# The last batch's dense pieces brought forward in an attention-and-experts kernel on one Trainium2 core

## The chip, the cores and the metric

The kernel runs on one core of one Trainium2 chip. The metric is the device time of one execution in microseconds (us); less is better. The core has five engines that run side by side, each through its own queue of instructions in order: TensorE (PE, matmuls), VectorE (DVE), ScalarE (ACT), GpSimd (POOL, here also the issuer of indirect transfers) and SyncE (SP, here the issuer of plain transfers). They wait for one another through semaphores.

## What is computed

The reference is block-sparse attention followed by a layer of dense and routed feed-forward parts. The kernel's change lies wholly in the second half, which the reference gives as:

```python
h_dense = np.maximum(x @ w1_dense, 0.0)
y_dense = h_dense @ w2_dense
logits = x @ w_gate
expert_idx = np.argmax(logits, axis=1)
...
for e in range(E):
    mask = expert_idx == e
    ...
    h = np.maximum(x[mask] @ w1[e], 0.0)
    y_moe[mask] = gate_w[mask, None] * (h @ w2[e])
return (y_dense + y_moe).astype(np.float32)
```

`x` is the attention's output, 3072 tokens of 512 values, in 4 batches of 768 tokens. There are 8 experts with 512 by 512 weights each. Each token goes to the expert with the highest logit. All inputs are random float32 values.

## The kernel before

The attention phase goes through 16 pairs of heads, four for each batch, in units that are written out by hand. When a batch's attention is done, its feed-forward work is given out in small pieces, called fills, between the units of the next batch: transposes, the gate, the ranks of the tokens within their experts, the dense pieces, and the scattering of the rows (`place`, line 370) into a table in HBM that is sorted by expert. Every row of that table carries the token's 512 values in half precision, its gate weight and its number.

The last batch has no next batch to hide in. Its pieces are given out in the experts' phase, which starts at line 675 and is the part that is changed.

The experts' phase goes through blocks of 128 table rows that all belong to one expert. There are at most 31 blocks (`NBLK`); 28 of them (`NOFT`) are run without a condition and three more behind a condition at the end. The first 11 (`N1`) are full blocks of the first three batches, so they can start before the last batch is routed. The other ones, the second part, need the last batch's rows in the table. The loop over `i` does this for each block, in this order:

- it fetches the rows of later blocks (`fetch`, line 454, tile `xg`, 14 buffers), up to eight blocks ahead (`AHEAD`), but no block of the second part before block `READY`
- `e1(i)`, line 699: four matmuls with the expert's first weights, then a ReLU on ScalarE into `eh`
- `tx(i + 1)`, line 691: four transposes of the next block's rows, then a copy on VectorE into `exT`
- the pieces of the last batch that `extra` holds for this block
- `e2(i - 1)`, line 728: four matmuls with the second weights, the scaling by the gate weight on VectorE into `yo` (line 735, four buffers), and on GpSimd an indirect transfer (line 736) that adds the 128 rows to the output at their tokens
- `th(i)`, line 708: four transposes of `eh`, then a copy on ScalarE into `ehT`

The last block of the loop gets the rows of the output beforehand (`dense_rows`, line 720, tile `dr`), adds them on VectorE (line 733) and writes the sum without accumulation.

There are 14 dense pieces of the last batch, in the list `d`: four `l1` and three `l2` for the first half of the batch, then the same for the second half. An `l1` (line 385) is four matmuls of 384 columns and a ReLU on ScalarE into a quarter of `hT` (line 387). An `l2` (line 394) reads all four quarters of `hT` for 128 tokens, is copied by ScalarE to `ys` (line 397), and SyncE stores `ys` to the output in two transfers of 64 rows (line 400). These stores overwrite, while line 736 adds. So an add must come after the store of the same token. The code frees the adds of the first 11 blocks from that wait, since they hold no token of the last batch:

```python
if i < N1:
    tc.declare_no_dep(sc.ins, group="dense", reason="the first blocks hold no token of the last batch")
    tc.add_to_no_dep_group("add1", sc.ins)
```

The adds from block 11 on wait for all dense stores of the last batch.

SyncE also writes zero rows behind each expert's rows in the table (`empty`, line 751) and loads the starting rows of the second part's 20 possible blocks into registers (`load_rows`, line 434), which is done when the loop comes to block `READY`. It does all this, the fetches and the stores in one queue, in the program's order. The tile framework may move instructions a little against the order in which the lines are called, but each engine runs its own list in order.

Of the kernel before, what the change touches and what calls it, by code (L numbers as in the profile page):

```python
# [17 lines left out]
def kernel(  # L18
# [38 lines left out]
    N1 = (N * (B - 1) // B - E * 127 + 127) // 128  # L57
# [388 lines left out]
    def load_rows(n):  # L446
        rows.extend(registers(ro[:, len(rows) : n], mybir.EngineType.SP, EMPTY,
                              "blocks lie in their expert's rows, or are the empty one"))
# [3 lines left out]
    def fetch(i):  # L452
        es[i]["x"] = xg = eg.tile([128, XW], U16, name="xg")
        ld = nc.sync.dma_start(out=xg, in_=table[bass.ds(rows[i], 128)])  # L454
        if i < N1:
            tc.add_to_no_dep_group("full", ld.ins)
# [218 lines left out]
    with (  # L675
# [8 lines left out]
        a, d, ranks, places, _ = batch_fills(B - 1)  # L684

        wef = we.rearrange("p e j f -> p (e j f)")
        def tx(i):
            s = es[i]
            tp = p1.tile([128, NK, 128], HF, name="tp", tag="tr")
            for ko in range(NK):  # L690
                nc.tensor.transpose(tp[:, ko], s["x"][:, ko * 128 : (ko + 1) * 128].bitcast(HF), ident)  # L691
            s["xT"] = xT = et.tile([128, NK, 128], HF, name="exT")
            nc.vector.tensor_copy(xT, tp)  # L693
# [21 lines left out]
        def dense_rows(i):  # L715

            es[i]["dense"] = dr = et.tile([128, Dm], FP, name="dr", bufs=1)
            nc.vector.memset(dr, 0.0)
            with tc.issue_after(latest["pool"].ins):
                ga = nc.gpsimd.indirect_dma_start(out=dr, out_offset=None, in_=out, in_offset=tokens(i),  # L720
                                                  bounds_check=N - 1, oob_is_err=False)
            apart(ga, "add", "every token is in one block")
# [30 lines left out]
                tc.declare_no_dep(z.ins, group="full", reason="the first blocks end before these rows")  # L753

        AHEAD = 8
        READY = 4
        tx(0)
        extra = {0: a[:NT] + [a[NT], ranks], 1: places[:2], 2: places[2:4], 3: places[4:] + [empty]}
        for n, f in enumerate(d):
            extra.setdefault(1 + n * (N1 - 2) // len(d), []).append(f)  # L760
        got = FIRST

        RARE = 3
# [1 line left out]
        for i in range(NOFT):  # L765
            if i == READY:
                load_rows(NBLK)
            while got < min(i + AHEAD + 1, NOFT if i >= READY else N1):
                fetch(got)
# [10 lines left out]
            if i == NOFT - 4:  # L780
                dense_rows(NOFT - 1)
            if i == READY + 1:
                total = nc.values_load_multi_w_load_instructions(
# [41 lines left out]
```

## Time and profile before

| | |
|---|---|
| time, median of 3 runs | 254.45 us (253.21 to 255.98) |
| span of the profiled execution | 252.1 us |
| TensorE busy | 216.1 us (86%) |
| VectorE busy | 176.7 us (70%) |
| ScalarE busy | 177.8 us (71%) |
| GpSimd busy | 158.8 us (63%) |
| first matmul of the experts (line 699) | at 167.80 us |
| scatter-adds (line 736) | 28, 1.55 us each, 43.3 us in all |

Times are counted from the start of the span. A line of the timeline gives the start, the length, the engine, the line of the code, the operation, the tile that is written and the tile that is read, and in brackets how long the engine stood idle before it and what ended that. In the row of a DMA issue the length is the issuing alone; the data land later. A releaser named in brackets is inferred from semaphores, and where an instruction waits for several of them only the last is named. "issue" in the chain of waits is time in which the engine waited for nothing that the profile shows.

### The profile page before, as it was taken

What the parts mean: (1) busy time and instruction counts of PE and PEld (TensorE: products, weight loads), DVE (VectorE), ACT (ScalarE), POOL (GpSimd) and SP (SyncE); (2) the same over time, 40 slices, a digit from 0 to 9 for tenths busy, and PEclk for the clock granted to TensorE, in tenths of its full rate; (3) what the DMA queues carried; (4) which work ended last, traced back from release to release, by engine and by line L of the source; (5) the groups of instructions that cost most, each with busy time, mean ns of one, the idle gap of its engine ahead of it and who ended that gap; (6) DMA issues with size and microseconds to landing.
All of it is one profiled execution on the core that took longest, in us unless ns stands there. A gap on an engine that the chain in (4) does not pass through costs nothing. (4 is left out here: it accounts for less than half of the span.)

```text
span 252.1 us, 7252 instructions
## 1 busy us (share of the span) xinstructions
PE 216.1 (86%) x2547; PEld 142.4 (56%) x2547; DVE 176.7 (70%) x558; ACT 177.8 (71%) x332; POOL 158.8 (63%) x198
## 2 busy tenths in 40 slices
PE   1389879788999999899999998979999999989970
PEld 0256646666756677766667764536555454545530
DVE  6968989999979599998599995138533344356540
ACT  2699989887778999778899876834556554545540
POOL 4746998767386687378678345501787452688882
PEclk9999999999999999999999999999999999999995
DMA  6999999999999999999899925275599999579786
GB/s 178 264 267 233 217 225 260 214 181 249 260 197 261 197 274 204 232 205 285 187 299 201 216 47 166 72 188 162 130 287 144 239 263 257 84 130 130 100 132 116
DMA packets 75125, 50.13 MB, mean 199 GB/s; under 512 B 29648, under 2 KB 68176, under 8 KB 75088
## 3 DMA queue, kind: packets, MB, share of 16 engines
q1 hardware_dynamic: 59856, 30.33, 47.4%
q0 software_dynamic: 15232, 19.32, 45.6%
q8 instruction: 21, 0.34, 0.5%
q14 instruction: 16, 0.13, 0.2%
HBM read 41.93 MB, written 18.23 MB: 239 GB/s over the span
## 5 line engine op out<-in xcount | busy, mean ns | idle before, releaser
L558 ACT ACTIVATE ex<-sp 128x512 f16<-128x512 f32 (+1 forms) x176 | 90.8, 602 | 2.7 <-PE op L573 1.8
L554 PE MATMUL sp<-rT,kT 128*128 128x128 f16 (+3 forms) x384 | 63.8, 261 | 4.5 <-ACT ex L558 3.1
L736 POOL DMA_INDIRECT out_dram<-yo,xg x28 | 43.3, 1546 | 20.1 <-DVE yo L735 8.1
L560 POOL TENSOR_SCALAR_AFFINE_SELECT ex<-ex 128x512 f16<-128x512 f16 x48 | 32.1, 681 | 35.6 <-ACT ex L558 33.6
L573 PE MATMUL op<-v,ex 128*128 128x65 f16 x672 | 44.6, 194 | 2.2 <-POOL ex L560 1.7
L573 PEld LDWEIGHTS <-ex 128*128 128x128 f16 x672 | 34.8, 98 | 15.0 <-POOL ex L560 5.3
L735 DVE TENSOR_SCALAR yo<-yp,xg 128x512 f32<-128x512 f32 x27 | 20.3, 750 | 24.9 <-PE yp L728 15.3
L370 POOL DMA_INDIRECT table<-xbig,slot x24 | 24.0, 1000 | 20.1 <-issue 19.5
L554 PEld LDWEIGHTS <-kT 128*128 128x128 f16 x384 | 28.7, 98 | 7.9 <-issue 5.4
L498 DVE TENSOR_REDUCE ks<-kp 128x24 f16<-128x768 f16 x30 | 27.3, 943 | 5.0 <-ACT kp L487 4.8
L699 PE MATMUL hp<-we,exT 128*128 x112 | 29.2, 379 | 1.5 <-DVE exT L693 1.5
L710 ACT COPY ehT<-tp 128x512 f16<-128x512 f16 x28 | 16.4, 586 | 19.9 <-PE tp L708 19.9
L728 PE MATMUL yp<-we,ehT 128*128 x112 | 28.7, 379 | 0.8 <-ACTq L788 0.8
L385 PE MATMUL hp<-xT,wd 128*128 128x384 f16 x128 | 26.2, 325 | 1.5 <-DVE xT L258 0.4
L394 PE MATMUL yp<-wd,hT 128*128 128x512 f16 x96 | 24.3, 378 | 2.2 <-ACT ys L397 1.8
L702 ACT ACTIVATE eh<-hp 128x512 f16<-128x512 f32 x28 | 16.7, 597 | 12.6 <-PE hp L699 12.6
L693 DVE COPY exT<-tp 128x512 f16<-128x512 f16 x28 | 11.8, 422 | 14.4 <-PE tp L691 14.4
L397 ACT COPY ys<-yp 128x512 f32<-128x512 f32 x24 | 14.3, 596 | 9.4 <-PE yp L394 9.1
L387 ACT ACTIVATE hT<-hp 128x384 f16<-128x384 f32 x32 | 15.9, 497 | 6.9 <-PE hp L385 6.8
L487 ACT COPY kp<-pp 128x768 f16<-128x768 f16 x16 | 12.9, 807 | 9.9 <-PE pp L485 9.8
L385 PEld LDWEIGHTS <-wd 128*128 128x128 f16 x128 | 12.0, 97 | 9.9 <-issue 4.7
L584 DVE TENSOR_TENSOR xbig<-op,rs 128x384 f16<-128x384 f32 x32 | 17.4, 548 | 0.2
(127 smaller groups left out, 385.1 us busy)
## 6 DMA issues: line engine op xcount, KB each, us to landing
we<-in_moe_w_dram POOLq DMA_DIRECT2D x16, 512.0 KB, 8.9
kf<-in_k_dram SPq DMA_DIRECT2D x32, 192.0 KB, 4.7
qf<-in_q_dram SPq DMA_DIRECT2D x32, 192.0 KB, 5.5
vf<-in_v_dram SPq DMA_DIRECT2D x32, 192.0 KB, 7.4
out_dram<-ys SPq DMA_DIRECT2D x48, 128.0 KB, 4.7
xg<-table SPq DMA_DIRECT2D x28, 136.0 KB, 3.4
table<-zt SPq DMA_DIRECT2D x9, 136.0 KB, 4.5
wd<-in_moe_w_dense_dram POOLq DMA_DIRECT2D x2, 512.0 KB
```

The costliest lines, as they stand in the source:

```text
L370: sc = nc.gpsimd.indirect_dma_start(out=table, out_offset=bass.IndirectOffsetOnAxis(ap=keep["slot"][:, t : t + 1], axis=0), in_=xbig[b % 2 ...
L385: nc.tensor.matmul(hp, wd[:, ko, j * 128 : (j + 1) * 128], xT[:, ko, g * G * 128 : (g + 1) * G * 128], start=(ko == 0), stop=(ko == NK - 1))
L394: nc.tensor.matmul(yp, hold["h"][:, j, i * 128 : (i + 1) * 128], wd[:, NK + j], start=(j == 0), stop=(j == NK - 1))
L498: nc.vector.tensor_reduce(out=ks[:, i], in_=kp.rearrange("d (c w) -> d c w", w=32), op=op, axis=mybir.AxisListType.X)
L554: nc.tensor.matmul(sp[:, o : o + w], kT[p % NB][g][:, kt * 128 : (kt + 1) * 128], rT[p % NB][g][:, a * 128 : z * 128], start=(o == 0), sto ...
L558: nc.scalar.activation(ex[:, 0:o], sp[:, 0:o], AF.Exp, scale=-0.125)
L560: latest["pool"] = nc.gpsimd.affine_select(out=ex, in_=ex, compare_op=ALU.is_ge, fill=0.0, base=0, pattern=[[0, 4], [1, 2], [2, 64]], chan ...
L573: nc.tensor.matmul(s["op", g][:, t * (D + 1) : (t + 1) * (D + 1)], ex[:, o : o + 128], v16[p % NB][:, g, kt, :], start=first, stop=(last_o ...
L699: nc.tensor.matmul(hp, s["xT"][:, ko], wef[:, bass.ds(offs[i] + ko * 512, 512)], start=(ko == 0), stop=(ko == NK - 1))
L728: nc.tensor.matmul(yp, s["hT"][:, j], wef[:, bass.ds(offs[i] + (NK + j) * 512, 512)], start=(j == 0), stop=(j == NK - 1))
L735: nc.vector.tensor_scalar(o, yp, gate, None, ALU.mult)
L736: sc = nc.gpsimd.indirect_dma_start(out=out, out_offset=to, in_=o, in_offset=None, bounds_check=N - 1, oob_is_err=False, compute_op=ALU.by ...
```

## The change

Two numbers in the experts' phase are changed.

```diff
         AHEAD = 8
-        READY = 4
+        READY = 6
         tx(0)
         extra = {0: a[:NT] + [a[NT], ranks], 1: places[:2], 2: places[2:4], 3: places[4:] + [empty]}
         for n, f in enumerate(d):
-            extra.setdefault(1 + n * (N1 - 2) // len(d), []).append(f)
+            extra.setdefault(1 + n * (READY - 1) // len(d), []).append(f)
```

The 14 dense pieces were spread over blocks 1 to 9, one or two in each. With the new formula they lie in blocks 1 to 5: three in each of the first four and two in the fifth. The register load of the second part's rows and the fetches of its blocks come at block 6 instead of block 4 (and the load of the number of blocks, line 783, at block 7 instead of 5), so that in SyncE's queue they lie behind the dense stores. At block 6 the fetches of blocks 11 to 14 come together, where before blocks 11 and 12 came at block 4 and one more with each block. The purpose is to have the last batch's dense rows in the output before the first add that must wait for them.

## The prediction

> **What bounds the kernel now.** I read the chain of waits first. It does not leave the last part of the experts' phase: from 205 us on it runs through scatter-adds of block outputs and nothing else of weight.
>
> ```profile
> 205.52 7.16 DMA out_dram<-yo,xg
> 212.78 2.03 DMA xg<-table
> 214.91 0.49 issue
> ...
> 217.49 3.94 DMA out_dram<-yo,xg
> ...
> 234.22 12.58 DMA out_dram<-yo,xg
> 246.81 0.11 POOLq L788
> 246.92 0.93 POOL out_dram L736
> ```
>
> The reader is to see the hole between 205.52 and 215. Next I read GpSimd (POOL) alone in order of time. It issues one scatter-add per block, and block 10 is the row at 207.88.
>
> ```profile
> 205.52 1.55 POOL L736 DMA_INDIRECT out_dram<-yo,xg  x1 [0.62 <-DVE yo L735]
> 207.88 1.57 POOL L736 DMA_INDIRECT out_dram<-yo,xg  x1 [0.81 <-DVE yo L735]
> 215.63 1.56 POOL L736 DMA_INDIRECT out_dram<-yo,xg  x1 [6.18 <-DMA xg<-table]
> 217.49 1.55 POOL L736 DMA_INDIRECT out_dram<-yo,xg  x1 [0.30 <-issue]
> ...
> 239.80 1.07 POOL L720 DMA_INDIRECT dr<-out_dram,xg  x1 [0.30 <-issue]
> ...
> 246.81 1.03 POOL L736 DMA_INDIRECT out_dram<-yo,xg  x1 [0.30 <-DMA out_dram<-yo,xg]
> ```
>
> The add at 215.63 is block 11's, the first that the code does not exempt from the last batch's dense stores (`i < N1`, N1 = 11). Its 6.18 us are put down to a fetch; by the code it must wait for the last dense store. SyncE's (SP) queue in order of time shows when those stores go out, and the answer for line 434 its register loads (least, median and longest ns):
>
> ```profile
> 191.24 1.12 SPq L400 DMA_DIRECT2D out_dram<-ys  x2
> 192.61 0.93 SPq L454 DMA_DIRECT2D xg<-table  x2
> ...
> 203.20 3.60 SPq L400 DMA_DIRECT2D out_dram<-ys  x4
> 207.05 1.23 SPq L454 DMA_DIRECT2D xg<-table  x2
> 208.38 1.12 SPq L400 DMA_DIRECT2D out_dram<-ys  x2
> ```
>
> ```profile
> L434 SPq TENSOR_LOAD <-ro x2: 1620/4234/6849, 151.3 to 184.3; - x2
> ```
>
> The last store is issued before 209.5; such a store takes 4.7 us to land (median, 7.8 at most, the answer for line 400), so about 214 to 216: this is the wait. From 215.63 on GpSimd runs adds back to back, 1.86 us each, to the end. TensorE (PE) is the other near bound: it is busy 9.1 to 10.0 us of every 10 from 170 to 240. It loses time in the second part here:
>
> ```profile
> 209.42 0.38 PE L708 MATMUL tp<-ident,eh 128*128 128x128 f16 x4 [0.62 <-PE yp L728]
> 220.34 0.75 DVE L735 TENSOR_SCALAR yo<-yp,xg 128x512 f32<-128x512 f32 x1 [2.47 <-DMA out_dram<-yo,xg]
> 221.56 1.02 PE L699 MATMUL hp<-we,exT 128*128 x4 [0.87 <-DVE exT L693]
> ```
>
> The late add of block 11 keeps one of the four `yo` buffers; VectorE (DVE) stands behind it for 2.47 us, the next `exT` copy is queued behind that, and TensorE waits 0.87 us.
>
> **What the Trainium skill says.** "DMA: Bandwidth & Descriptors", section "Issuing engines are not separate DMA queues": transfers of all issuers share the same 16 engines and interleave. The trace agrees: the DMA share is 1.0 or more in most 2 us stretches from 182 to 214, and fetches that land in 2.1 us at best take 5 to 7.7 us there. "Runtime: NRT & Kernel Launch", section "Instruction fetch mechanics": a register load costs some 200 ns per register, which makes 4 us an estimate for the 20 of the second part. The trace differs both ways: 11 values took 1.62 us (147 ns each) with the DMA nearly idle, 20 took 6.85 us (342 ns each) in the saturated stretch. The measured pair is my bound: 2.9 to 6.85 us.
>
> **The change part by part.**
> *Dense pieces.* There are 14: eight `l1` (187.14 to 187.79 in the trace, 0.65 us of TensorE each) and six `l2` (180.21 to 181.07, 0.86 us). Their sum, 10.4 us, stays. By the formula they stood 2, 2, 1, 2, 1, 2, 1, 2, 1 in blocks 1 to 9; now they stand 3, 3, 3, 3, 2 in blocks 1 to 5. A block without pieces takes 2.18 us (line 699 at 204.51 and again at 206.69). So line 699 of block 2 moves from 175.61 to about 176.26, and blocks 3, 4, 5, 6 begin near 180.9, 185.2, 189.7 and 193.6 (before 179.12, 182.16, 186.06, 188.88). With 2.18 us each, block 11 begins at 204.5: where it begins now. No gain and no loss, because TensorE is full in both. Two new places, in blocks 2 and 4, put an `l2` right behind the `l1` whose `hT` its last matmul reads: ScalarE's 0.49 us against three matmuls of 0.22 us, about 0.15 us each; 0 to 0.4 us together, taken 0.3 and already in these sums. ScalarE gets 1.2 us plus at most 1.8 us in a block of over 4 us: hidden.
>
> *Stores.* The last two `l2` now end near 192.5, with copies done by 193.3. In SyncE's queue of the changed kernel the twelve stores stand before every second-part fetch; three are behind the load of the 20 registers. SyncE comes to that load near 187.4 (seven zero fills at 0.5 to 0.6 us and six stores of the first three pieces at about 0.55 us from 180 on). It ends between 190.3 and 194.3; I take 192.9, nearer the slow one, since the stretch is as saturated. Six stores at 0.55 us end near 196.3. With 5 to 7.8 us they have landed by 204. Block 11's add is ready only near 210. The 6.18 us wait goes entirely.
>
> *Fetches.* This is the added wait. Block 11's fetch is issued at about 196.4 instead of 192.61, and may be as early as 194.9 or as late as 197.8. Right behind stores such a fetch took up to 7.7 us, otherwise 5.3: it lands between 200.2 and 205.5. TensorE wants it at 203.2 (before the transposes of block 11 that stand in block 10), and everything on TensorE is queued behind that. Cost 0 to 2.3 us; I take 0.4 (196.4 plus 7 to 7.2). The other fetches follow 0.6 us apart or after stores have landed, and are wanted 2.18 us apart: hidden.
>
> *What is won at the end.* From 204.51 to line 699 of block 27 at 241.12 are 36.6 us for 16 blocks, 34.8 at 2.175: 1.8 us lost in the two waits above and beside them. Of these the 0.87 goes surely, and the 0.62 probably (it lies behind an expert register load of 1.27 us in the saturated stretch, which is over earlier now); 1.6 taken. Then GpSimd's lag: the last `yo` is done at 245.97, its add starts at 246.81, 0.84 late. Without the hole GpSimd needs 1.86 us against TensorE's 2.18, so it never falls behind but for the gather for `dr` (1.07 plus 0.31) after block 23's add; that leaves 1.07, 0.75, 0.54, 0.34 in the next four. Gain 0.5. Sum: 1.6 + 0.5 - 0.4 = 1.7 us. The profiled run took 253.8 us, the median is 254.45; the wait that goes depends on DMA timing, so the slower runs may hold more of it, and some of the difference falls away too. I forecast 252.2 us.
>
> **Rivals.**
> 1. *The fetch is late.* The new wait takes the place of the old. For it: the fetch loses 4 to 5 us of a slack of about 5. Against: this needs both the slow load and the slow landing. With the 2.3 us bound: 254.45 - 2.1 + 2.3 = 254.6. With every store at the slowest 1.29 us seen (line 400 reaches 2.4) the fetch goes 3 to 4 us later than taken and TensorE waits 5 us or so: 254.45 - 2.1 + 5 = 257.3, slower than before.
> 2. *The wait was hidden anyway.* Adds catch up 0.3 us a block, and only 0.84 us of lag was left; if TensorE's two waits have other DMA causes, only the 0.5 is won: 254.0. Against: the chain from the late add through VectorE to TensorE at 220 to 221.6 is plain.
> 3. *More is won.* All 1.8 us, no late fetch, no saturated tail, and the runs at 256 gone with the store wait: 2.3 plus 0.8, or 251.3.
>
> **How the numbers follow.** Forecast (251.4 to 253.2): 0.50, of which nearly half lies under 251.9. More won: 0.20. Late fetch at 254 to 255: 0.11. Hidden: 0.08. Slower, near 257: 0.11. One per cent of 254.45 is 2.5 us, so the lines are 251.9 and 257.0. Under 251.9 lie 0.20 and 0.22 of the forecast; over 257.0 lie 0.08 of the last. The range leaves out that case and the rim of the third rival: 250.7 to 255.0.
>
> **What would show it.** Right: the wait ahead of block 11's add under 1 us; adds in the second part about 2.18 us apart and waiting for `yo`; no `yo` waiting on an add; block 27's line 699 near 239.6; the last dense store issued before 198. Wrong: TensorE waiting for `xg` at block 11's transposes for more than 1 us; the register load over 7 us; or adds still 1.86 us apart to the end.

## The result, and the profile after

The change makes the kernel slower: 261.57 us (median of 4 runs, 261.20 to 261.91) against 254.71 us (4 runs, 253.21 to 255.98) for the kernel before on the same chip. The ratio is 1.0271 with a 95% interval of [1.0213, 1.0330]. The prediction was 252.2 us. Some executions of each of these kernels take over 1.5% longer than the fastest of the same kernel; all ratios in this document leave those out, while medians and spreads hold all runs.

In the profiled execution of the kernel after, the attention phase ends later too: the first expert matmul stands at 170.44 us instead of 167.80. So times of the two profiles are compared from that matmul on ("after the first expert matmul"), and the stretch from it to the end of the span is called the phase. The table has it in parts, each from the start of line 699 of one block to that of another.

| us | first expert matmul | phase | blocks 0 to 6 | 6 to 11 | 11 to 27 | 27 to end |
|---|---|---|---|---|---|---|
| before | 167.80 | 84.3 | 21.08 | 15.63 | 36.60 | 10.98 |
| after | 170.44 | 89.8 | 25.91 | 17.20 | 35.44 | 11.21 |

The chain of waits of the kernel after, in order of time (start, length, what), around the place where the old one had its hole:

```profile
199.77 0.88 PE yp L728 x4
...
201.82 0.79 SPq L400
202.66 1.53 SPq L400
204.43 6.54 DMA xg<-table
211.01 0.61 PE tp L691 x4
```

It no longer runs through a late scatter-add. It runs through two dense stores in SyncE's queue (SPq), then the fetch behind them, then TensorE. The same place in TensorE's timeline (start, length, engine, line, operation, tiles, count, idle before and releaser):

```profile
206.27 1.03 PE L699 MATMUL hp<-we,exT 128*128 x4
211.01 0.61 PE L691 MATMUL tp<-ident,xg 128*128 128x128 f16 x4 [3.72 <-DMA xg<-table]
211.41 1.91 PE L728 MATMUL yp<-we,ehT 128*128 x4
213.12 0.64 PE L708 MATMUL tp<-ident,eh 128*128 128x128 f16 x4
213.55 1.21 PE L699 MATMUL hp<-we,exT 128*128 x4
```

Block 11's transposes (line 691) are due when block 10's four matmuls at 206.27 have been issued. They start at 211.01, when block 11's rows have come. Then two things are to be seen: the wait of 3.72 us, and that the groups after it are slow, 1.91 us where the group before the wait took 1.03. SyncE's queue and its register loads (line 434: least, median and longest ns) show why the rows came late:

```profile
183.16 1.41 SPq L751 DMA_DIRECT2D table<-zt  x3
184.67 3.23 SPq L400 DMA_DIRECT2D out_dram<-ys  x4
188.10 3.51 SPq L751 DMA_DIRECT2D table<-zt  x4
191.71 12.48 SPq L400 DMA_DIRECT2D out_dram<-ys  x8
204.43 24.53 SPq L454 DMA_DIRECT2D xg<-table  x17
```

```profile
L434 SPq TENSOR_LOAD <-ro x2: 1607/3807/6007, 153.9 to 192.9; - x2
```

The row at 191.71 is eight stores, and the register load (6.007 us, at 192.94) lies inside it, after the second store. The fetch of block 11 heads the last row. From the first expert matmul it is issued 34.0 us on, where the kernel before issued it after 24.8. Last, GpSimd's scatter-adds, from block 8's on:

```profile
207.28 1.55 POOL L736 DMA_INDIRECT out_dram<-yo,xg  x1 [1.58 <-DVE yo L735]
214.40 1.55 POOL L736 DMA_INDIRECT out_dram<-yo,xg  x1 [5.57 <-DVE yo L735]
217.09 1.57 POOL L736 DMA_INDIRECT out_dram<-yo,xg  x1 [1.15 <-DVE yo L735]
219.08 1.56 POOL L736 DMA_INDIRECT out_dram<-yo,xg  x1 [0.42 <-DVE yo L735]
...
225.60 1.55 POOL L736 DMA_INDIRECT out_dram<-yo,xg  x1 [0.62 <-DVE yo L735]
...
254.26 1.03 POOL L736 DMA_INDIRECT out_dram<-yo,xg  x1 [0.30 <-DVEq L788]
```

The hole of 5.57 us now stands ahead of block 9's add: block 9's second four matmuls come behind block 11's transposes in TensorE's list, and so wait with them. Block 11's own add is the row at 219.08. It waits 0.42 us for its `yo` and no longer for the dense stores. From there on the adds stand mostly 2.17 us apart and wait for `yo`, that is for TensorE, up to the gather for `dr`. What the change was made for has happened, and it cost more than it brought.

### The profile page after: what moved, and what is told of

Its sections match the earlier page's. It is cut to its first block, busy times and chain, and to the rows that moved or that the text cites. A ratio compares the mean times of both kernels' runs of the same rounds, so it can differ in the third digit from the quotient of the medians.

```text
span 260.2 us, 7253 instructions
## 1 busy us (share of the span) xinstructions
PE 218.3 (84%) x2547; PEld 143.0 (55%) x2547; DVE 176.6 (68%) x558; ACT 177.9 (68%) x332; POOL 159.0 (61%) x198
## 4 chain that ended last, share of the span: by engine, by line
PE 33%; DMA 20%; DVE 18%; ACT 11%; POOL 7%; issue 5%; SPq 2%; POOLq 0%; ACTq 0%; DVEq 0%
PE hp L385 7%; DMA qf<-in_q_dram 6%; DMA xg<-table 6%; PE yp L394 5%; DMA out_dram<-yo,xg 5%; ACT ex L558 4%; PE yp L728 4%; POOL out_dram L736 4%; PE hp L699 4%; DVE ks L498 4%; PE sp L554 3%; DMA out_dram<-ys 3%; ACT hT L387 2%; ACT ys L397 2%; PE op L573 2%
## 5 line engine op out<-in xcount | busy, mean ns | idle before, releaser
L736 POOL DMA_INDIRECT out_dram<-yo,xg x28 | 43.2, 1544 | 24.8 <-DVE yo L735 20.2
L560 POOL TENSOR_SCALAR_AFFINE_SELECT ex<-ex 128x512 f16<-128x512 f16 x48 | 32.2, 683 | 35.3 <-ACT ex L558 32.2
L370 POOL DMA_INDIRECT table<-xbig,slot x24 | 24.1, 1004 | 20.6 <-issue 19.6
L728 PE MATMUL yp<-we,ehT 128*128 x112 | 29.6, 388 | 0.8 <-ACTq L788 0.8
L474 POOL CAST q<-qf 128x768 f16<-128x768 f32 x16 | 13.3, 829 | 8.4 <-DMA qf<-in_q_dram 7.9
```

What stands on the lines that cost most here:

```text
L370: sc = nc.gpsimd.indirect_dma_start(out=table, out_offset=bass.IndirectOffsetOnAxis(ap=keep["slot"][:, t : t + 1], axis=0), in_=xbig[b % 2 ...
L560: latest["pool"] = nc.gpsimd.affine_select(out=ex, in_=ex, compare_op=ALU.is_ge, fill=0.0, base=0, pattern=[[0, 4], [1, 2], [2, 64]], chan ...
L728: nc.tensor.matmul(yp, s["hT"][:, j], wef[:, bass.ds(offs[i] + (NK + j) * 512, 512)], start=(j == 0), stop=(j == NK - 1))
L736: sc = nc.gpsimd.indirect_dma_start(out=out, out_offset=to, in_=o, in_offset=None, bounds_check=N - 1, oob_is_err=False, compute_op=ALU.by ...
```

## The experiments

Three causes were weighed. The first (A in the expectations) is the queue: block 11's fetch stands behind the 20-register load and the stores, and TensorE waits for it. The second is that one half of the change does harm by itself; the expectations name the early packing of the dense pieces (B). The third (C) is that the loss lies outside the experts' phase, in the 2.6 us of the attention phase.

**Each half alone.**

```diff
 # e1_pieces_only: READY stays 4
-            extra.setdefault(1 + n * (N1 - 2) // len(d), []).append(f)
+            extra.setdefault(1 + n * 5 // len(d), []).append(f)
 # e2_ready_only: the pieces stay
-        READY = 4
+        READY = 6
```

> The dense pieces in blocks 1 to 5 as in the changed kernel, but READY = 4 as before: in SyncE's queue the fetches of blocks 11 and 12 come right behind the register load, ahead of three pairs of dense stores. Theory A (the loss is TensorE waiting for block 11's rows, whose fetch stands behind the 6 us register load and three pairs of stores): the fetch goes out some 5 us earlier, TensorE waits less than 1 us for it, and the time falls to 253 to 257 us. Theory B (the early packing itself slows TensorE and floods the DMA engines, the fetch is a symptom): it stays at 259 to 262 us. Theory C (2.7 us of the loss arise by chance in the attention phase, whose first expert matmul is at 170.44 instead of 167.80 us): the first expert matmul is again near 170.4 in some kernels and near 167.8 in others, whatever the edit, and the times differ by as much.

> READY = 6 alone, the dense pieces spread over blocks 1 to 9 as before. The register load stands where it stood, but three pairs of stores now come ahead of block 11's fetch. Theory A: the fetch is issued about 4 us later than before, at 196 to 198 us against the 203 us at which it is wanted plus 5 to 7.7 us of landing: TensorE waits 0 to 2 us; the add of block 11 still waits for the last dense store; 255 to 257.5 us. Theory B: 254 to 255.5 us, as before. Theory C: as for the first kernel.

Measured: 0.9999 [0.9966, 1.0031] for the pieces alone and 1.0013 [0.9968, 1.0058] for the later release alone. Neither loses. In SyncE's queue of the kernel with the pieces alone, the fetches of blocks 11 and 12 go out before the last six stores:

```profile
190.99 1.47 SPq L400 DMA_DIRECT2D out_dram<-ys  x2
198.42 0.91 SPq L454 DMA_DIRECT2D xg<-table  x2
199.44 1.11 SPq L400 DMA_DIRECT2D out_dram<-ys  x2
```

The hole in front of the fetches (from 192.46 to 198.42) is the register load (5.64 us here), and block 11's fetch is issued 29.0 us after the first expert matmul. With the later release alone it is 28.6 us, the load 6.64 us. With the pieces alone, six of the twelve stores and the load stand ahead of the fetch; with the later release alone, the load and six stores. Only the whole change puts the load and all twelve stores there, and the fetch is then issued at 34.0 us. So the harm is in the sum of the two.

**After, with a short load.** The loop loads four of the 20 values first and the other 16 after the stores; the order of stores and fetches is that of the kernel after, held there by further lines that are left out here. Line numbers are shifted by the edits: in this kernel 756 is a zero fill, 459 a fetch, and 696 and 704 are what 691 and 699 were.

```diff
-            if i == READY:
-                load_rows(NBLK)
             # in the loop that fetches ahead:
+                if got == N1:
+                    load_rows(N1 + 4)
+                elif got == N1 + 4:
+                    with tc.issue_after(latest["store"].ins):
+                        load_rows(NBLK)
```

> The changed kernel, with the register load ahead of the stores cut from 20 values to 4 (plus the one of the number of blocks); the other 16 are loaded behind the first four fetches of the second part. The fetches still stand behind all dense stores. Theory A: the load takes 1 to 2 us instead of 6, so block 11's fetch goes out 3 to 5 us earlier and TensorE waits 0 to 1 us: 253.5 to 257 us. If the stores alone are what delays the fetch, TensorE still waits 3 us or more and the time is 259 to 261 us. Theory B: 259 to 262 us.

Measured: 0.9986 [0.9942, 1.0030]. The four values took 2.29 us. SyncE's queue, and TensorE at block 11's transposes (the row at 205.97):

```profile
187.15 3.85 SPq L756 DMA_DIRECT2D table<-zt  x4
191.09 7.71 SPq L400 DMA_DIRECT2D out_dram<-ys  x8
199.06 13.02 SPq L459 DMA_DIRECT2D xg<-table  x12
```

```profile
205.11 1.03 PE L704 MATMUL hp<-we,exT 128*128 x4
205.97 0.39 PE L696 MATMUL tp<-ident,xg 128*128 128x128 f16 x4
```

All eight stores and the load now take 7.71 us instead of 12.48, the fetch still stands behind every store, and it is issued 29.1 us after the first expert matmul. TensorE does not wait for it: blocks 6 to 11 take 11.55 us instead of 17.20. That settles the first cause against the second, and it says which part of the queue matters: the same stores stand ahead of the fetch, the load is 3.7 us shorter and the stores together 1.1 us quicker, and the whole loss is gone. The third cause falls as an explanation of the whole loss: this kernel's first expert matmul is at 169.92, nearly as late as after's, and its time is that of the kernel before. The kernel with the later release alone has it at 172.14.

**Stores through ScalarE's queue.** The last batch's stores leave SyncE's queue, so that the fetch stands behind the load alone.

```diff
+                    eng = nc.scalar if b == B - 1 else nc.sync
-                    st_ = nc.sync.dma_start(out=outv[m, j], in_=ys[64 * j : 64 * j + 64])
+                    st_ = eng.dma_start(out=outv[m, j], in_=ys[64 * j : 64 * j + 64])
```

> The changed kernel, with the last batch's twelve dense stores issued by ScalarE, right after its own copies, instead of SyncE. SyncE's queue holds the zero fills, the register load and the fetches alone. Theory A: the register load begins 3 us earlier or more and block 11's fetch follows it at once: no wait of TensorE for it, and no wait of block 11's add for the stores; 252 to 256 us. ScalarE issues 12 transfers of about 0.5 us, 6 us in all, beside TensorE's work in blocks of over 4 us; if that delays the copies TensorE waits for, 1 to 2 us more. Theory B: 259 to 262 us.

Measured: 1.0271 [1.0104, 1.0439], a miss. The fetch is indeed early (25.5 us after the first expert matmul) and blocks 6 to 11 take 11.28 us, but blocks 0 to 6 take 32.34. The timeline of ScalarE and TensorE at the place (401 is the store, 703 the ReLU into `eh`):

```profile
187.70 1.91 ACTq L401 DMA_DIRECT2D out_dram<-ys  x2
189.65 0.60 ACT L703 ACTIVATE eh<-hp 128x512 f16<-128x512 f32 x1 [6.13 <-issue]
190.30 1.44 PE L385 MATMUL hp<-xT,wd 128*128 128x384 f16 x4 [4.64 <-ACT eh L703]
```

ScalarE was free for the second pair of stores at 183.5. In the trace every plain transfer, of SyncE or of ScalarE, uses one of the same eight semaphores, and in the rows here its issuer waits for that semaphore first. The semaphore of this store had last been used by one of SyncE's zero fills; that fill was issued at 182.26 and landed at 187.62, and the store's wait ended at 187.64. The ReLU into `eh` is queued behind the store, and TensorE, which lost 4.64 us here, behind the ReLU.

**The rows loaded four at a time**, each load just before the fetches that need it, otherwise with the lines of the kernel after. (Here and below, a line behind the loop that loads what is left over is not shown.)

```diff
-            if i == READY:
-                load_rows(NBLK)
             # in the loop that fetches ahead:
+                if got == len(rows):
+                    load_rows(min(got + 4, NBLK))
```

> The dense pieces in blocks 1 to 5, READY = 6, but the 20 starting rows are loaded four at a time, each ahead of the fetches that use them; in SyncE's queue the first four fetches then stand behind a load of 4 values and ahead of three pairs of stores. Theory A (the fetch's place behind the 6 us load and the stores is the loss): no wait of TensorE for block 11's rows; from the first expert matmul to the end 83 to 84.5 us (before 84.3, changed kernel 89.8, pieces alone 84.5, short load 83.5). The times: 253 to 256 us, as far as the attention phase, which begins the experts between 167.8 and 172.1 us in the profiles so far, lets one see it. Theory B (the early packing is slow in itself): 88 us or more for the phase.

Measured: 0.9961 [0.9930, 0.9992]. The five loads took 1.52 to 2.22 us each, and block 11's fetch is issued 26.7 us after the first expert matmul. The order in SyncE's queue is not that of the kernel after: the first four fetches go out ahead of the last six stores. The phase is 84.7 us in its profile, no shorter than the 84.3 of before.

**After again, and TensorE kept busy in the wait.** The kernel after was run once more, on another chip, and beside it with 110 matmuls of 56 columns into a scratch tile, put on TensorE ahead of block 11's transposes. They add nothing to the output.

```diff
+            if i == N1 - 1:
+                fill = p4.tile([128, NT + 1, E], FP, name="fill", tag="rk")
+                for _ in range(FILL):
+                    nc.tensor.matmul(fill, ones, ones[:, 0 : (NT + 1) * E], start=True, stop=True, skip_group_check=True)
```

> The changed kernel once more, unedited, on the chip of these runs. Theory A: the wait of TensorE for block 11's rows comes again, 3 to 5 us, and the phase takes 89 to 91 us wherever the attention phase ends; the time is 4 to 7 us over that of before. Theory C (chance in the attention phase makes the loss): the phase takes the same, but the time over before falls to about 5 us when the attention phase ends early.

> The changed kernel with 110 small matmuls (56 columns, about 0.027 us each, 3 us together, into a scratch tile) put on TensorE just ahead of block 11's transposes, where it waits 3.9 us for the rows. They add nothing to the output. If the clock that fell to 0.52 to 0.62 in the 4 us after the wait fell because TensorE stood idle, it stays near 1.0 now, the matmuls behind the wait take 1.03 us a group instead of 1.2 to 1.9, and the phase takes 88.3 to 89 us instead of 89.8. If it fell for another reason, the phase takes 89.5 to 91 us.

Measured: 1.0125 [1.0022, 1.0227] for after again (4 runs from 256.98 to 265.61), 1.0213 [1.0135, 1.0291] with the filler; the two intervals overlap, so the times don't tell what the filler is worth. The profiles do. After again has the same wait:

```profile
209.33 0.61 PE L691 MATMUL tp<-ident,xg 128*128 128x128 f16 x4 [4.32 <-DMA xg<-table]
```

The busy time of the first profile of the kernel after (the one with the wait of 3.72 us), by stretches of 2 us, and then one stretch of the kernel with the filler (columns: stretch, length, busy TensorE, weight loads, VectorE, ScalarE and GpSimd with counts, granted TensorE clock, DMA share, GB/s):

```profile
208.00:210.00 2.00, 0.00 (x0) 0.00 (x0) 0.00 (x0) 0.00 (x0) 0.83 (x1) 1.00 1.02 233
210.00:212.00 2.00, 0.99 (x6) 0.71 (x7) 0.34 (x1) 0.00 (x0) 0.00 (x0) 0.62 1.07 260
212.00:214.00 2.00, 2.00 (x10) 0.93 (x8) 0.72 (x2) 0.15 (x1) 0.00 (x0) 0.52 1.07 294
214.00:216.00 2.00, 2.00 (x17) 1.17 (x16) 0.66 (x3) 1.03 (x2) 1.55 (x1) 1.00 0.84 280
```

```profile
210.00:212.00 2.00, 1.90 (x15) 1.15 (x16) 1.03 (x2) 0.33 (x1) 0.00 (x0) 1.00 1.12 276
```

After the idle stretch the granted clock is 0.62 and then 0.52; with the filler it stays at 1.00 at the same place. TensorE's timeline with the filler (776 is the filler):

```profile
206.81 3.00 PE L776 MATMUL fill<-ones 128*128 128x56 f16 x110
210.10 0.40 PE L691 MATMUL tp<-ident,xg 128*128 128x128 f16 x4 [0.28 <-DMA xg<-table]
210.33 1.03 PE L728 MATMUL yp<-we,ehT 128*128 x4
```

From line 699 of block 10 to that of block 11 it is 5.47 us instead of 7.28, 1.8 less. Part of that is a fetch that came a little earlier here (210.10 - 206.81 = 3.3 us from the start of the wait, against 3.9 after); the other 1.2 us are the clock.

**Two pieces per block, in blocks 1 to 7, and the two parts of that.** The release stays at block 4. The fetches then stand among the stores and not behind them, and the last store goes out 39.3 us after the first expert matmul, a little before the 41.1 of the kernel before.

```diff
 # e8_two_per_block: both; e9_two_whole_load: the formula alone; e10_spread_by_4: the loads alone
-            extra.setdefault(1 + n * (N1 - 2) // len(d), []).append(f)
+            extra.setdefault(1 + n // 2, []).append(f)
-            if i == READY:
-                load_rows(NBLK)
+                if got == len(rows):
+                    load_rows(min(got + 4, NBLK))
```

> Two dense pieces per block in blocks 1 to 7, READY = 4, the starting rows loaded four at a time. Less packed than the changed kernel, the last dense store some 8 us before block 11's add instead of behind it. Theory A: neither wait; the phase takes 82.8 to 84 us, the time 253 to 255.5 us. Theory B predicts no worse than the kernel before, so it says the same here. If the gain of the second part (1.1 to 1.4 us in the two kernels without either wait) is always lost to TensorE's own register loads in blocks 6 to 10, the phase takes 83.8 to 84.5 us.

> Two dense pieces per block in blocks 1 to 7 and READY = 4, with the 20 starting rows loaded at once as before. In SyncE's queue block 11's fetch stands behind the load and two pairs of stores. If the spacing of the pieces is what makes the kernel with two per block and loads of four good (82.9 us from the first expert matmul to the end), this one takes 82.8 to 84 us; if the short loads do it, 84 to 85 us. No wait of TensorE for block 11's rows in either case, since the fetch goes out some 27 us after the first expert matmul and is wanted at 36.

> The kernel before with nothing changed but the 20 starting rows loaded four at a time. The last dense store is still issued 40 us after the first expert matmul or a little earlier, so block 11's add still waits for it, 3 to 5 us. If that wait costs the 1.1 us by which the second part is shorter in the kernels without it, the phase takes 83.8 to 84.5 us; if short loads alone help, 83.5 us or less.

Measured: both 0.9955 [0.9916, 0.9995]; the formula alone 0.9974 [0.9937, 1.0011]; the loads alone 1.0026 [0.9988, 1.0064]. The loads of the first took 0.87 to 2.33 us, and block 11's fetch is issued 22.5 us after the first expert matmul. GpSimd's adds from block 10 on:

```profile
208.37 1.57 POOL L736 DMA_INDIRECT out_dram<-yo,xg  x1 [0.80 <-DVE yo L735]
214.11 1.56 POOL L736 DMA_INDIRECT out_dram<-yo,xg  x1 [4.17 <-DMA xg<-table]
215.98 1.55 POOL L736 DMA_INDIRECT out_dram<-yo,xg  x1 [0.31 <-DVE exT L693]
```

Block 11's add still waits 4.17 us, and yet the phase is 82.9 us, the shortest but one of all. In the kernel with the loads alone it waits longer (add, then block 15's `yo`, which needs its buffer, then TensorE):

```profile
217.16 1.56 POOL L736 DMA_INDIRECT out_dram<-yo,xg  x1 [6.58 <-DMA xg<-table]
...
221.75 0.75 DVE L735 TENSOR_SCALAR yo<-yp,xg 128x512 f32<-128x512 f32 x1 [3.02 <-DMA out_dram<-yo,xg]
...
222.97 1.02 PE L699 MATMUL hp<-we,exT 128*128 x4 [1.44 <-DVE exT L693]
```

So an add could be about 4 us late here before TensorE felt much of it; at 6.58 TensorE loses 1.44 us in one place. From the first expert matmul to the end, the profile with the formula alone has 84.3 us and the one with the loads alone 86.1, which is longer than expected. These are single profiles, and the intervals of the times overlap, so which of the two parts brings the gain is not shown.

**The best once more**, unedited, in more rounds.

> The kernel with two dense pieces per block and loads of four once more, for a narrower interval. If its gain of 0.45% is real, the ratio to the kernel before lies between 0.993 and 0.998 and the phase takes 82.5 to 83.5 us; if it was chance, 0.998 to 1.002 and 83.5 to 84.5 us.

Measured: 254.42 us (median of 22 runs), 0.9958 [0.9929, 0.9987]. It is 0.4% faster than the kernel before and, by the ratios of the kernel after on the two chips, 1.6 to 3% faster than that one. Its phase is 82.9 us again. The kernel with the pieces in blocks 1 to 5 and loads of four (0.9961) is as good within the intervals.

## Why the prediction was wrong

The profiles differ by 8.1 us of span. 2.6 of them lie ahead of the experts' phase, in code that the change doesn't touch; the same kernel after had its first expert matmul at 170.44 in one profile and at 168.23 in the other. In the 13 profiles of all kernels it lies between 167.7 and 172.1 us. So they are taken as scatter of the attention phase. The phase itself is 5.5 us longer:

- *Dense pieces*: right. Block 6 was to begin 193.6 - 167.8 = 25.8 us after the first expert matmul; it begins after 25.91.
- *Stores*: right in what matters. The last one was issued 32.2 us after the first expert matmul, later than the sign named (before 198 - 167.8 = 30.2), but block 11's add waits 0.42 us, and none of that for a store.
- *Blocks 6 to 11*: these should have given the 4.7 us back (block 11 was to begin where it had), and took 1.6 more instead, 6.3 us off. By TensorE's timeline, 3.9 are the wait for `xg` (to 211.01 from 207.14, where the next group would follow block 10's matmuls at the usual 0.87 us), 1.2 the lower clock behind it (from 211.01 to 213.55, 2.54 us where 1.30 is usual), and 1.2 two long blocks before, 2.45 and 3.13 us instead of 2.17. In these TensorE's queue has register loads of its own (0.81 and 1.49 us), with no dense piece left to lie over them. The short-load kernel has the last part too (2.71 and 2.32).
- *Blocks 11 to 27*: 1.2 us won, where 1.6 were taken. *The end*: 0.2 lost, where 0.5 of gain was taken. GpSimd's lag is as worked out (last `yo` done at 253.85, its add at 254.26, 0.41 against 0.34 predicted), and its add starts 5.27 us after block 27's first matmul, where before it was 5.69; but from that add to the end of the span it is 5.9 us instead of 5.3.

The step that failed is *Fetches*, and in it one term: "Cost 0 to 2.3 us; I take 0.4". It was 3.9 us of waiting, and 5.1 with the slow clock behind it. The prediction's own first sign of being wrong, TensorE waiting for `xg` at block 11's transposes, is what the trace shows. The mechanism was named and priced, as rival 1; the issue time of the fetch was mis-sized. From the first expert matmul:

| | predicted | measured |
|---|---|---|
| SyncE comes to the register load | 19.6 | 22.5 |
| length of the load | 5.5 | 6.0 |
| six stores, from the load's end to the fetch | 3.4 to 3.5 | 5.5 |
| fetch of block 11 issued | 28.6 | 34.0 |
| fetch lands after | 7 to 7.2 | 6.54 |
| TensorE wants it | 35.4 | 36.7 |

The load itself, on which the range was built, was 0.5 us off. The landing was even shorter than taken. Of the other 4.9 us, 0.5 are a later start of the zero fills (12.7 instead of 12.2), and 4.4 are issues in SyncE's queue that took longer than the 0.5 to 0.6 us taken for each: one store took 1.39, two zero fills 1.46 and 0.83, two of the last stores 1.04 and 1.53. The rows 184.67, 188.10 and 191.71 in SyncE's queue show their sums. The trace of before had that in sight: four stores in 3.60 us at 203.20, and a slowest of 2.4. It was used in rival 1 only, which came to "5 us or so" and 257.3; wait and clock together were 5.1. That the two agree is partly luck: the wait alone was 3.9, and the clock was not in the rival. Nor did it need the slow landing that the prediction held against it. The bound of the term should have held such slow issues.

Three parts were not foreseen. One is stated in the Trainium skill and had no place in the prediction: "TensorE: Matmul & The Clock Gate", Part 1 on the clock gate, says that an idle window of some 3.4 us halves TensorE's clock and that it takes about as long of work to get it back. The trace agrees: after 3.72 us of idling the clock is 0.62 and 0.52 and full again from 214 on, and 1.44 us of idling, in the kernel with the loads alone, left it at 1.00. The second is the exposed register loads. The third is how little the old wait was worth. With it gone and no late fetch (pieces alone, short load), the time is that of before, within the intervals; against the short load's profile, blocks 11 to 27 give 1.4 us and blocks 0 to 11 take 0.7 back. Rival 2, the wait hidden anyway, had that half right: four `yo` buffers hide some 4 us of lateness.

What stays open: why single transfers on SyncE take up to 1.5 us to issue there (2.0 us in the kernel with the pieces alone). In the slow store at 202.66 the transfer that it had to wait for had landed by 195.3, so that wait is not it; nothing here separates the rest. Also open is how often the fetch is so late, and with it the size of the loss: the kernel after ran only eight times, from 256.98 to 265.61 us over the two chips, while the kernel before, run many more times beside the experiments, reached 261.71 us too. Both profiles of the kernel after show the wait; the run of 256.98 us was not profiled.

## What to carry to other kernels

Ask of each transfer what stands ahead of it in its issuer's queue, and add that up with the slowest issues that the trace shows in the same kind of stretch, not the usual ones; a register load and stores that are each harmless ahead of a fetch were not so together. Where a long register load stands ahead of a fetch that an engine will soon wait for, cutting it can be enough: here it took away the whole loss. Where the fetch had time to spare, cutting it gained nothing (1.0026). A wait of an engine off the critical path is worth only what its buffers don't hide, while a wait of nearly 4 us on TensorE cost about a third more than its length here, by the clock.

## What the runs showed of the hardware

- *Clock.* After 3.7 us (after) and 4.3 us (after again) without matmuls, groups of four took up to 1.91 us instead of 1.03; matmuls without use in the wait kept the clock at 1.00.
- *Register loads.* 11 values took 1.6 us where the DMA was nearly idle; 20 values took 5.6 to 6.9 us in the saturated stretch; four values took 0.87 to 2.43 us on SyncE in the same part of the kernel. "Runtime: NRT & Kernel Launch", section "Instruction fetch mechanics", has some 200 ns per register. The page describes such loads as reading HBM, and these read a small tile on the chip. The runs lie at up to 147 with a nearly idle DMA, at 278 to 342 for the 20 values, and between 217 and 608 for the four. Five loads of four took 7.5 to 8.6 us together, so here the one long load is the cheaper one in sum and was still the worse one ahead of a fetch.
- *Transfers from a compute engine's queue.* A store on ScalarE stood 4.1 us (183.5 to 187.6) for the landing of a SyncE transfer that had used the same semaphore before, and compute behind it stood with it.
